# Moving the last quarter of a weight load, and its matmuls, behind the last attention unit of a decode kernel

## The chip, the cores and the metric

The kernel runs on one core of one Trainium2 chip. Times are device microseconds (us) of that core for one execution. Most executions of one kernel lie within about 1 us of each other, with now and then one 2 to 3.5 us above the fastest. So differences under half a microsecond are never read from times here, only from where instructions and transfers stand in the traces.

## The reference, cut to what matters

One decode step of a transformer block: batch 4, one new token, 32 heads of width 192, a cache of 4096 positions, model width 640, feed-forward width 1536, all bf16.

```python
q = layernorm(x) @ wq                                # 640 -> 32 x 192
p = softmax(q . k_cache * 192 ** -0.5)               # for each of 4 x 32 (batch, head)
h = x + (p @ v_cache) @ wo                           # 6144 -> 640
g = layernorm(h)
out = h + (silu(g @ w_gate) * (g @ w_up)) @ w_down   # 640 -> 1536 -> 640
```

K and V are 403 MB of the 424 MB that the kernel reads. Each byte is used once.

## The kernel before

The work is cut into 32 *units* of one batch row and four heads. A unit needs one 6.3 MB load of K and one of V. Two K buffers and one V buffer lie in on-chip memory; weights are laid over the buffers when these come free. SP (the sync engine) issues all large loads on one queue (q1, 424.29 of the 424.48 MB that the profile counts); a helper records operations with their dependences and puts the waits in. `wo` is used by *head pairs*: 16 pairs of 12 small matmuls each.

The end of the queue, in the order in which it is issued:

```python
# wo_a (pairs 0..11) over K buffer 0, wo_b (pairs 12..15) over the product buffers
for lo, hi, t, deps in ((0, WA, woA, [lambda: tk["tt", NU - 2, NQ - 1]]),
                        (WA, P, woB, [lambda: tk["red", NU - 1, NQ - 1]])):
    a = dma("sp", ... t <- wo[pairs lo..hi] ..., deps)
load_v(NU - 1)                 # last V, in four pieces, each with a semaphore of its own
k_free = [lambda: tk["tt", NU - 1, NQ - 1]]
wg_land = dma("sp", ... wgsb <- wg ..., k_free)      # gate, 2 MB
wu_land = dma("sp", ... wusb <- wu ..., k_free)      # up, 2 MB
for lo, hi in ((0, 6), (6, 10), (10, CF)):           # down, 2 MB in three pieces
    t = dma("sp", ... wdsb[:, lo:hi] <- wd ..., k_free)
```

The end of the tensor engine's (PE's) program, which PE carries out in order (queue_only, below, shows it: PE stood 12.81 us in front of one group of matmuls with the operands of the next already there):

```python
u = NU - 1
for p in range(P - 2):         # 14 head pairs: all units but the last row are done
    womm(p)
l_sum(u)
for lo, hi in VP:              # the last unit's p times V, piece by piece
    pv(u, lo, hi)
tmp(u); stt(u); o_t(u); recip(u); otm(u)     # merge, transpose, scale into OTall
womm(P - 2)                    # the two pairs that need the last unit
wo_done = womm(P - 1)
ln2 = layer_norm(psH[:, 0:DQ], [wo_done])
# ... wg's 20 matmuls [ln2, wg_land], wu's 20 matmuls [ln2, wu_land],
# ... gate product, transpose, wd's 48 matmuls by piece [wd_land], copy, output
```

## Time and profile before

| | before |
|---|---|
| time, median of 4 runs | 994.04 us (993.87 to 994.43) |
| span of the profiled execution | 992.2 us |
| mean DMA rate over the span | 428 GB/s |
| PE busy, DVE (vector engine) busy | 58%, 56% |

From the page of the profile: the span; the DMA row of the 40 slices, where 9 means 90% busy or more; the rates in those slices; and queue 1, which carries the large loads, with packets, MB and the share of 16 engines' span.

```profile
span 992.2 us, 9305 instructions
...
DMA  9999999999999999999999999999999999999997
GB/s 402 427 436 433 423 438 438 420 442 436 420 444 434 422 444 430 426 440 430 430 440 428 432 440 424 432 442 422 436 440 422 438 438 422 440 436 420 421 417 306
...
q1 hardware_dynamic: 12608, 424.29, 99.3%
q8 instruction: 7, 0.11, 0.0%
q14 instruction: 8, 0.07, 0.0%
```

The stream of loads is full from start to end, and only the last slice shows a gap. So the question for any change is what it does to the bytes or to the microseconds after the last bytes.

The last lines of the page: size of each load and microseconds from issue to landing.

```profile
wo_a<-in_A_wo_dram SPq DMA_DIRECT2D x1, 5760.0 KB, 39.5
v<-in_A_v_cache_dram SPq DMA_DIRECT2D x1, 3072.0 KB, 20.6
wo_b<-in_A_wo_dram SPq DMA_DIRECT2D x1, 1920.0 KB, 13.7
wg_sb<-in_B_w_gate_dram SPq DMA_DIRECT2D x1, 1920.0 KB, 28.7
wu_sb<-in_B_w_up_dram SPq DMA_DIRECT2D x1, 1920.0 KB, 32.1
```

The timeline of the tail: start, duration, engine, line, operation, and in brackets the engine's idle time before it and what ended it. PEld is the load of weights into PE.

```profile
946.78 0.38 SPq L365 DMA_DIRECT2D wo_b<-in_A_wo_dram  x1
947.21 3.88 SPq L354 DMA_DIRECT2D v<-in_A_v_cache_dram  x4
...
975.31 0.81 PE L455 MATMUL pb<-v,pbuf 128*8 128x384 bf16 x8 [1.37 <-DMA v<-in_A_v_cache_dram]
...
978.46 0.97 PE L495 MATMUL pb<-wo_b,OTall 128*4 128x160 bf16 x24 [0.55 <-DVE OTall L486]
...
979.48 0.33 DVE L294 BATCH_NORM_STATS2 stats<-pb 128x6 f32<-128x160 f32 x1 [0.21 <-PE pb L495]
...
982.83 1.77 PE L551 MATMUL pb<-wg_sb,lnT 128*4 128x384 bf16 x20 [1.90 <-DVE lnT L308]
...
984.49 0.10 PEld L551 LDWEIGHTS pb<-wu_sb,lnT 128*4 128x4 bf16 x8 [0.61 <-DMA wu_sb<-in_B_w_up_dram]
984.50 1.77 PE L551 MATMUL pb<-wu_sb,lnT 128*4 128x384 bf16 x20
...
987.88 1.77 PE L561 MATMUL pb<-wd_sb,guT 128*4 128x160 bf16 x48 [1.61 <-DVE guT L557]
989.70 0.33 DVE L564 CAST outsb<-pb 128x160 bf16<-128x160 f32 x1 [1.88 <-PE pb L561]
```

Issue time plus time to landing gives wo_b 946.78 + 13.7 = 960.5, wg 951.13 + 28.7 = 979.8 and wu 952.33 + 32.1 = 984.4. The reader should see two clocks running to the same point. One is work: last V, merge, `wo`, layer norm, wg's matmuls, until PE is ready for wu at about 984.5. The other is the stream, which delivers wu at 984.4. Their ends coincide.

### The profile page before, as it was taken

The numbers are of one execution on the slowest core, as the hardware profiler recorded it, in microseconds if no ns is written. First come the engines' busy times: TensorE is split into PE (matmuls) and PEld (weight loads), VectorE is DVE, ScalarE is ACT, GpSimd is POOL, SyncE is SP. The second block draws the span as 40 slices with busy tenths as digits, with TensorE's granted clock in tenths as the row PEclk, the third lists the DMA queues.
The fourth block names the chain that finished last, engine by engine and source line by source line (L and its number), as shares of the span: only waits on it lengthen the run. The fifth ranks groups of instructions, "written<-read, shape, count | busy, mean of one in ns | idle before, by whom it ended". The sixth has DMA issues, their size and how long they took to land.

```text
span 992.2 us, 9305 instructions
## 1 busy us (share of the span) xinstructions
PE 577.5 (58%) x4656; PEld 117.2 (12%) x3248; DVE 552.7 (56%) x451; ACT 108.0 (11%) x348; POOL 3.4 (0%) x19
## 2 busy tenths in 40 slices
PE   0766555676555566655557655555665555666545
PEld 0101111111001111001111100111110011110032
DVE  1486645566654556664555666455666545566602
ACT  0311111110011110001111000111100111110011
POOL 1000000000000000000000000000000000000000
PEclk9788778887777888777788877788887778887775
DMA  9999999999999999999999999999999999999997
GB/s 402 427 436 433 423 438 438 420 442 436 420 444 434 422 444 430 426 440 430 430 440 428 432 440 424 432 442 422 436 440 422 438 438 422 440 436 420 421 417 306
DMA packets 12671, 424.48 MB, mean 428 GB/s; under 512 B 1264, under 2 KB 1264, under 8 KB 3952
## 3 DMA queue, kind: packets, MB, share of 16 engines
q1 hardware_dynamic: 12608, 424.29, 99.3%
q8 instruction: 7, 0.11, 0.0%
q14 instruction: 8, 0.07, 0.0%
q10 hardware_dynamic: 48, 0.01, 0.0%
HBM read 424.29 MB, written 0.01 MB: 428 GB/s over the span
## 4 chain that ended last, share of the span: by engine, by line
DMA 67%; PE 18%; DVE 13%; SPq 1%; issue 0%; ACT 0%; DVEq 0%
DMA k<-in_A_k_cache_dram 60%; PE pb L152 11%; DVE prod L403 11%; DMA v<-in_A_v_cache_dram 8%; PE pb L455 5%; PE pb L411 2%; DVE sc L416 1%; SPq L350 0%; PE pb L551 0%; SPq L354 0%; PE pb L561 0%; PE pb L495 0%; DVE guT L557 0%; PE pb L480 0%; PE pb L298 0%
## 5 line engine op out<-in xcount | busy, mean ns | idle before, releaser
L403 DVE TENSOR_TENSOR prod<-k,qball 128x6144 f16<-128x6144 bf16 x128 | 426.3, 3351 | 200.8 <-DMA k<-in_A_k_cache_dram 200.8
L152 PE MATMUL pb<-prod,identH 128*128 128x512 f16 x1408 | 385.8, 431 | 0.0
L411 PE MATMUL pb<-prod,identH 128*128 128x512 f16 x128 | 57.9, 452 | 340.5 <-DVE prod L403 334.2
L416 DVE TENSOR_REDUCE sc<-pb 128x32 f32<-128x512 f32 x128 | 88.0, 688 | 114.0 <-PE pb L152 114.0
L455 PE MATMUL pb<-v,pbuf 128*8 128x384 bf16 x2048 | 90.8, 330 | 9.2 <-DMA v<-in_A_v_cache_dram 9.1
L461 ACT ACTIVATE otmp<-pb,mask 128x192 f32<-128x192 f32 x32 | 13.4, 420 | 678.2 <-PE pb L455 678.2
L411 PEld LDWEIGHTS pb<-prod,identH 128*128 128x128 f16 x128 | 13.2, 103 | 588.0 <-DVE prod L403 466.7
L444 ACT ACTIVATE pbuf<-sc,negM 32x128 bf16<-32x128 f32 x128 | 73.4, 574 | 2.7 <-ACT negM L438 0.2
L455 PEld LDWEIGHTS pb<-v,pbuf 128*8 128x8 bf16 x2048 | 46.8, 87 | 121.3 <-DMA v<-in_A_v_cache_dram 86.6
L465 DVE SCALAR_TENSOR_TENSOR orow<-pb,mask,otmp 128x192 f32<-128x192 f32 x32 | 13.4, 418 | 77.4 <-ACT otmp L461 77.4
L444 ACT ACTIVATION_READ_ACCUMULATOR pbuf<-sc,negM 32x1 f32 x128 | 31.7, 248 | 0.0
L480 PE MATMUL pb<-pick,orow 128*64 128x2 f32 x384 | 22.3, 231 | 2.9 <-DVE orow L465 1.0
L438 ACT ACTIVATE negM<-pb 128x4 f32<-128x4 f32 x32 | 5.5, 173 | 161.1 <-PE pb L434 161.1
L470 PEld LDWEIGHTS pb<-lsb,halfm 128*128 128x128 f32 x64 | 12.1, 190 | 72.1 <-issue 71.1
L480 PEld LDWEIGHTS pb<-pick,orow 128*64 128x64 f32 x384 | 19.6, 174 | 6.2 <-DVE orow L465 1.7
L434 PE MATMUL pb<-negMc,ones_row 1*128 1x4 f32 x64 | 12.2, 258 | 11.9 <-DVE negMc L429 11.9
L429 DVE TENSOR_REDUCE negMc<-pb 1x4 f32<-1x128 f32 x32 | 8.9, 279 | 15.1 <-PE pb L425 15.1
L425 PE MATMUL pb<-identF,msb 128*1 128x128 f32 x64 | 12.2, 271 | 8.3 <-DVE msb L421 8.2
L298 PE MATMUL pb<-mv,quadm 128*128 128x2 f32 x4 | 1.2, 364 | 23.5 <-DVE mv L296 23.5
L434 PEld LDWEIGHTS pb<-negMc,ones_row 1*128 1x128 f32 x64 | 9.4, 183 | 21.3 <-DVE negMc L429 21.3
L294 DVE BATCH_NORM_STATS2 stats<-xrow 128x6 f32<-128x160 bf16 x1 | 0.3, 327 | 17.6 <-DMA xrow<-in_A_x_dram 17.6
L495 PE MATMUL pb<-wo_a,OTall 128*4 128x160 bf16 x144 | 5.2, 335 | 7.9 <-DMA wo_a<-in_A_wo_dram 6.7
(66 smaller groups left out, 92.0 us busy)
## 6 DMA issues: line engine op xcount, KB each, us to landing
k<-in_A_k_cache_dram SPq DMA_DIRECT2D x32, 6144.0 KB, 39.9
v<-in_A_v_cache_dram SPq DMA_DIRECT2D x31, 6144.0 KB, 25.7
wq_sb<-in_A_wq_dram SPq DMA_DIRECT2D x1, 7680.0 KB, 21.2
wo_a<-in_A_wo_dram SPq DMA_DIRECT2D x1, 5760.0 KB, 39.5
v<-in_A_v_cache_dram SPq DMA_DIRECT2D x1, 3072.0 KB, 20.6
wo_b<-in_A_wo_dram SPq DMA_DIRECT2D x1, 1920.0 KB, 13.7
wg_sb<-in_B_w_gate_dram SPq DMA_DIRECT2D x1, 1920.0 KB, 28.7
wu_sb<-in_B_w_up_dram SPq DMA_DIRECT2D x1, 1920.0 KB, 32.1
```

Source lines behind the costliest of these rows:

```text
L152: return e.add_instruction(mybir.InstMatmult(name=e.bass.get_next_instruction_name(), engine=mybir.EngineType.PE, start_tensor_calc=start, ...
L403: op("dve", lambda e: e.tensor_tensor(out=prod[BUF[k]][:, :, :], in0=kslot[u % 2][:, k * QT:(k + 1) * QT, :], in1=qball[:, u, None, :].bro ...
L411: op("pe", lambda e, j=j: (e.matmul if j == 0 else partial(held_matmul, e))(psR[k][:, 0:QT * R], lhsT=identH[:, :], rhs=prod[BUF[k]][:, :, ...
L416: op("dve", lambda e: e.tensor_reduce(sc[u % 2][:, k * QT:(k + 1) * QT], psR[k][:, 0:QT * R].rearrange("q (t r) -> q t r", r=R), AX.X, ALU ...
L425: op("pe", lambda e: e.matmul(psS[0:1, XT], lhsT=msb[:, 0:1], rhs=identF[:, :], start=True, stop=True), [g("rmax", u), g("negM", u - 1), p ...
L434: op("pe", lambda e: e.matmul(psS[:, XB], lhsT=ones_row[0:1, :], rhs=negMc[0:1, :], start=True, stop=True), [g("hmax", u), g("negM", u - 1 ...
L444: op("act", lambda e, h=h, r=r: e.activation(out=pbuf[r, :, h], in_=sc[u % 2][r, :], func=ACTF.Exp, bias=negM[r, h:h + 1], scale=alpha, ac ...
L455: op("pe", lambda e, t=t, n=n: e.matmul(psO[32 * n:32 * n + 8, 0:2 * DH], lhsT=pbuf[:, t:t + 2, :].rearrange("q t m -> q (t m)"), rhs=vslo ...
L461: op("act", lambda e: e.activation(out=otmp[:, :], in_=psO[:, 0:DH], func=ACTF.Copy, scale=mask[:, 0:1]), [g("pv", u), g("stt", u - 1), km ...
L465: op("dve", lambda e: e.scalar_tensor_tensor(out=orow[:, :], in0=psO[:, DH:2 * DH], scalar=mask[:, 1:2], in1=otmp[:, :], op0=ALU.mult, op1 ...
L470: op("pe", lambda e: e.matmul(psL[:, XL], lhsT=halfm[:, :], rhs=lsb[:, :], start=True, stop=True), [g("exp", u), g("otm", u - 1)], key=("l ...
L480: op("pe", lambda e, j=j, s=s, lo=lo: e.matmul(psL[64 * s:64 * s + 64, lo:lo + 2], lhsT=orow[:, j:DH:3], rhs=pick[:, s:4:2], start=True, s ...
```

## The change

The intent: when the last V arrives behind wo_b, it arrives later than it could, by the time of wo_b's 1.97 MB (4.8 us by the landings, 955.7 to 960.5), and a long chain of work hangs on it. So the last V goes ahead of wo_b in the queue, and the matmuls of wo_b's four pairs go behind the last unit's on PE, so that they don't hold it up. The core of the diff:

```diff
-    wo_land = []
-    for lo, hi, t, deps in ((0, WA, woA, ...), (WA, P, woB, ...)):
-        ...
-    load_v(NU - 1)
+    load_wo(0, WA, woA, [lambda: tk["tt", NU - 2, NQ - 1]])
+    if LATE:
+        load_v(NU - 1)
+    load_wo(WA, P, woB, [lambda: tk["red", NU - 1, NQ - 1]])
+    if not LATE:
+        load_v(NU - 1)
...
-    for p in range(P - 2):
+    early = WA if LATE else P - 2          # 12 instead of 14
+    for p in range(early):
         womm(p)
     ...
-    womm(P - 2)
-    wo_done = womm(P - 1)
+    for p in range(early, P):
+        wo_done = womm(p)
```

Cut: the file also brings switches that are off (a faster query projection, and `LOOPS`, which rolls the unit loops of the vector and scalar engines as the PE loop already is), a new layout of OTall, `[pair, j, batch]` becoming `[unit, 2, j]`, so that the slices of OTall, which PE loads as the stationary operand of `wo`'s matmuls, are read with a step of 6 elements, and a rewritten rule for the waits inside a rolled loop. Apart from the moved operations, the order of instructions is the same on every engine.

More of the change, by code (lines that the diff above doesn't have):

```diff
@@ L12 @@
 FP16 = mybir.dt.float16
-ROLL = True
+LOOPS = False
+FASTQ = False
+LATE = True
+HELD = False
 class Cfg:
@@ L46, in __init__ @@
         self.rolled = {}
+        self.shift = 0
     def op(self, eng, fn, deps=(), key=None):
@@ L112, in body @@
                     a, n, count = at[first], at[first + 1] - at[first], last - first
-                    delta = []
+                    plan = []
                     for j in range(n):
-                        w = [waits[a + s * n + j] for s in range(count)]
-                        d = [v - w[0][m][1] for m, (_, v) in enumerate(w[1])]
-                        for s in range(count):
-                            assert at[first + s] == a + s * n
-                            assert ops[a + s * n + j].needed == ops[a + j].needed
-                            assert [(k.name, v) for k, v in w[s]] == [
-                                (k.name, v + s * d[m]) for m, (k, v) in enumerate(w[0])], (j, s, w[0], w[s])
-                        delta.append(d)
+                        w = [{k.name: (k, v) for k, v in waits[a + s * n + j]} for s in range(count)]
+                        now = []
+                        for name in sorted(set().union(*w)):
+                            k, last = w[-1][name]
+                            d = last - w[-2][name][1]
+                            v = last - (count - 1) * d
+                            assert v > 0
+                            for s in range(count):
+                                assert at[first + s] == a + s * n
+                                assert ops[a + s * n + j].needed == ops[a + j].needed
+                                assert name not in w[s] and s < 2 or w[s][name][1] == v + s * d, (eng, j, s, name)
+                            now.append((k, v, d))
+                        plan.append(now)
                     for t, w in zip(ops[:a], waits[:a]):
@@ L127, in body @@
                     with self.nc.Fori(0, count, 1, engines=bass.OrderedEngineSet([e.engine]),
-                                      head_slot={e.engine: 0}) as s:
+                                      head_slot={e.engine: 0} if eng == "pe" else None) as s:
+                        self.shift = s
                         for j in range(n):
-                            for (k, v), d in zip(waits[a + j], delta[j]):
+                            for k, v, d in plan[j]:
                                 e.wait_ge(k, s * d + v)
                             one(e, ops[a + j])
+                        self.shift = 0
                     i = a + n * count
@@ L147, in emit, with held_matmul @@
         block.sync(run("sp"))
-def held_matmul(e, out, lhsT, rhs, start, stop):
+def held_matmul(e, out, lhsT, rhs, start, stop, size=(128, 128), position=(0, 0)):
     return e.add_instruction(mybir.InstMatmult(
         name=e.bass.get_next_instruction_name(), engine=mybir.EngineType.PE, start_tensor_calc=start,
-        stop_tensor_calc=stop, tile_size=(128, 128), tile_position=(0, 0), ldweights=False,
+        stop_tensor_calc=stop, tile_size=size, tile_position=position, ldweights=False,
         ins=[e.lower_ap(rhs), e.lower_ap(lhsT, for_matmul_weights=True)], outs=[e.lower_ap(out)]))
@@ L201, in build_kernel @@
     pbuf = sb("pbuf", [128, T, 4], BF16)
-    OTall = sb("OTall", [128, P, 3, B], BF16)
+    OTall = sb("OTall", [128, NU, 2, 3], BF16)
     qsb = sb("qsb", [128, 4, 2 * DH], BF16)
-    sel = sb("sel", [128, B, 32], BF16)
+    sel = sb("sel", [128, B, 128 if FASTQ else 32], BF16)
     identF = sb("identF", [128, 128], FP32)
@@ L282, in build_kernel @@
     op("dve", lambda e: e.memset(epsv[:, :], eps))
-    ksel = op("dve", lambda e: e.tensor_copy(
-        out=sel[:, :, :], in_=r32[:, 0:B][:, :, None].broadcast_to([128, B, 32])), [c1])
+    if FASTQ:
+        ksel = op("dve", lambda e: e.tensor_copy(
+            out=sel[:, :, :].rearrange("q b (h i) -> q b h i", h=4),
+            in_=identF[:, :].rearrange("q (h r) -> q r h", h=4)[:, 0:B, :, None].broadcast_to([128, B, 4, 32])), [c2])
+    else:
+        ksel = op("dve", lambda e: e.tensor_copy(
+            out=sel[:, :, :], in_=r32[:, 0:B][:, :, None].broadcast_to([128, B, 32])), [c1])
     kquad = op("dve", lambda e: e.tensor_scalar(
@@ L321, in build_kernel @@
     qcopy = []
-    for k in range(4):
+    if FASTQ:
         for c in range(CD):
-            for n in range(4):
-                p = 2 * (4 * (k // 2) + n) + k % 2
-                a = op("pe", lambda e, k=k, c=c, n=n, p=p: e.matmul(
-                    PB[k][32 * n:32 * n + B, 0:2 * DH], lhsT=lnT[:, c, 0:B],
-                    rhs=wqsb[:, c, p * 2 * DH:(p + 1) * 2 * DH], start=(c == 0), stop=(c == CD - 1)),
-                    [ln1, wq_land, zp])
-        qcopy.append(op("act", lambda e, k=k: e.activation(
-            out=qsb[:, k, :], in_=PB[k][:, 0:2 * DH], func=ACTF.Copy, scale=1.0), [a]))
+            for k in range(4):
+                for n in range(4):
+                    rhs = wqsb[:, c, 8 * k * DH:8 * (k + 1) * DH].rearrange("q (s d) -> q s d", s=2)[:, :, n * DH:(n + 1) * DH]
+                    mm = partial(held_matmul, size=(128, 32), position=(0, 32 * n)) if k and HELD else lambda e, *a, **kw: e.matmul(*a, **kw)
+                    a = op("pe", lambda e, k=k, c=c, n=n, rhs=rhs, mm=mm: mm(
+                        e, PB[k][32 * n:32 * n + B, 0:2 * DH], lhsT=lnT[:, c, 0:B], rhs=rhs,
+                        start=(c == 0), stop=(c == CD - 1)), [ln1, wq_land, zp])
+                if c == CD - 1:
+                    qcopy.append(op("act", lambda e, k=k: e.activation(
+                        out=qsb[:, k, :], in_=PB[k][:, 0:2 * DH], func=ACTF.Copy, scale=1.0), [a]))
+    else:
+        for k in range(4):
+            for c in range(CD):
+                for n in range(4):
+                    p = 2 * (4 * (k // 2) + n) + k % 2
+                    a = op("pe", lambda e, k=k, c=c, n=n, p=p: e.matmul(
+                        PB[k][32 * n:32 * n + B, 0:2 * DH], lhsT=lnT[:, c, 0:B],
+                        rhs=wqsb[:, c, p * 2 * DH:(p + 1) * 2 * DH], start=(c == 0), stop=(c == CD - 1)),
+                        [ln1, wq_land, zp])
+            qcopy.append(op("act", lambda e, k=k: e.activation(
+                out=qsb[:, k, :], in_=PB[k][:, 0:2 * DH], func=ACTF.Copy, scale=1.0), [a]))
     wq_used = a
@@ L362, in build_kernel, with load_wo @@
             load_k(u + 2)
-    wo_land = []
-    for lo, hi, t, deps in ((0, WA, woA, [lambda: tk["tt", NU - 2, NQ - 1]]), (WA, P, woB, [lambda: tk["red", NU - 1, NQ - 1]])):
-        a = dma("sp", lambda e, lo=lo, hi=hi, t=t: e.dma_start(
+    wo_land = {}
+    def load_wo(lo, hi, t, deps):
+        a = dma("sp", lambda e: e.dma_start(
             t[:, :, :, :].rearrange("q p j n -> q p (j n)"),
             wo[lo * 2 * DH:hi * 2 * DH, :].rearrange("(p q j) n -> q p (j n)", q=128, j=3)), sem(f"s_wo{lo}"), deps)
-        wo_land += [a] * (hi - lo)
-    load_v(NU - 1)
+        for p in range(lo, hi):
+            wo_land[p] = a
+    load_wo(0, WA, woA, [lambda: tk["tt", NU - 2, NQ - 1]])
[4 more added lines that the diff above has]
+        load_v(NU - 1)
     k_free = [lambda: tk["tt", NU - 1, NQ - 1]]
@@ L383, in build_kernel @@
     qbc = {}
-    for i in range(NU // 2):
-        c = i * 2 // B
-        n, bank = c % 4, psQ[i % 2]
-        for s in range(2):
-            b = (2 * i + s) % B
-            for h in range(4):
-                k, lo = 2 * (c // 4) + h // 2, (h % 2) * DH
-                a = op("pe", lambda e, bank=bank, s=s, b=b, h=h, n=n, k=k, lo=lo: e.matmul(
-                    bank[32 * h:32 * h + 32, s * DH:(s + 1) * DH], lhsT=sel[32 * n:32 * n + B, b, :],
-                    rhs=qsb[32 * n:32 * n + B, k, lo:lo + DH], start=True, stop=True),
-                    [qcopy[k], qcopy[-1], ksel, qbc.get(i - 2)])
-        qbc[i] = op("act", lambda e, i=i, bank=bank: e.activation(
-            out=qball[:, 2 * i:2 * i + 2, :].rearrange("q u d -> q (u d)"), in_=bank[:, 0:2 * DH],
-            func=ACTF.Copy, scale=QS), [a])
+    if FASTQ:
+        for i in range(NU // 2):
+            k, b, bank = i // B, i % B, psQ[i % 2]
+            a = op("pe", lambda e, bank=bank, k=k, b=b: e.matmul(
+                bank[:, 0:2 * DH], lhsT=sel[:, b, :], rhs=qsb[:, k, :], start=True, stop=True),
+                [qcopy[k], qcopy[-1], ksel, qbc.get(i - 2)])
+            qbc[i] = op("act", lambda e, k=k, b=b, bank=bank: e.activation(
+                out=qball[:, 8 * k + b:8 * k + b + B + 1:B, :], in_=bank[:, 0:2 * DH].rearrange("q (s d) -> q s d", s=2),
+                func=ACTF.Copy, scale=QS), [a])
+    else:
+        for i in range(NU // 2):
+            c = i * 2 // B
+            n, bank = c % 4, psQ[i % 2]
+            for s in range(2):
+                b = (2 * i + s) % B
+                for h in range(4):
+                    k, lo = 2 * (c // 4) + h // 2, (h % 2) * DH
+                    a = op("pe", lambda e, bank=bank, s=s, b=b, h=h, n=n, k=k, lo=lo: e.matmul(
+                        bank[32 * h:32 * h + 32, s * DH:(s + 1) * DH], lhsT=sel[32 * n:32 * n + B, b, :],
+                        rhs=qsb[32 * n:32 * n + B, k, lo:lo + DH], start=True, stop=True),
+                        [qcopy[k], qcopy[-1], ksel, qbc.get(i - 2)])
+            qbc[i] = op("act", lambda e, i=i, bank=bank: e.activation(
+                out=qball[:, 2 * i:2 * i + 2, :].rearrange("q u d -> q (u d)"), in_=bank[:, 0:2 * DH],
+                func=ACTF.Copy, scale=QS), [a])
     BUF = (0, 1, 2, 0)
@@ L404, in tt @@
             out=prod[BUF[k]][:, :, :], in0=kslot[u % 2][:, k * QT:(k + 1) * QT, :],
-            in1=qball[:, u, None, :].broadcast_to([128, QT, DH]), op=ALU.mult),
-            [landed["k", u], qbc[u // 2], last], key=("tt", u, k))
+            in1=qball[:, bass.ds(u + 2 * pr.shift, 1), :].broadcast_to([128, QT, DH]), op=ALU.mult),
+            [landed["k", u], qbc[NU // 2 - 1 if FASTQ else u // 2], last], key=("tt", u, k))
     def red(u, k):
@@ L484, in otm @@
     def otm(u):
-        c, b = u // B, u % B
         op("dve", lambda e: e.tensor_tensor(
-            out=OTall[:, 2 * c:2 * c + 2, :, b], in0=psL[:, XO].rearrange("q (j a) -> q a j", a=2),
+            out=OTall[:, bass.ds(u + 2 * pr.shift, 1), :, :].rearrange("q u a j -> q (u a) j"), in0=psL[:, XO].rearrange("q (j a) -> q a j", a=2),
             in1=invL[:, :, None].broadcast_to([128, 2, 3]), op=ALU.mult),
@@ L495, in womm @@
                 a = op("pe", lambda e, j=j, n=n: e.matmul(
-                    psH[32 * n:32 * n + B, 0:DQ], lhsT=OTall[:, p, j, :],
+                    psH[32 * n:32 * n + B, 0:DQ], lhsT=OTall[:, p // 2 * B:p // 2 * B + B, p % 2, j],
                     rhs=w[:, p if p < WA else p - WA, j, n * DQ:(n + 1) * DQ], start=False,
@@ L502, in build_kernel @@
         pr.step("pe")
+        if u % 2 == 0:
+            pr.step("dve")
+            pr.step("act")
         for k in range(NQ):
@@ L525, in build_kernel @@
             otm(u - 1)
-    pr.step("pe")
-    if ROLL:
-        pr.roll("pe", 2, NU)
+    for eng in ("pe", "dve", "act"):
+        pr.step(eng)
+    pr.roll("pe", 1 if FASTQ else 2, NU)
+    if LOOPS:
+        pr.roll("dve", 1, NU // 2)
+        pr.roll("act", 1, NU // 2)
     u = NU - 1
     load_act = op("act", lambda e: e.activation(out=mv[:, 3:4], in_=epsv[:, 0:1], func=ACTF.Sqrt))
-    for p in range(P - 2):
+    early = WA if LATE else P - 2
+    for p in range(early):
         womm(p)
```

## The prediction

> **What bounds the kernel now.** The DMA stream. The page gives DMA queue q1 99.3% of the span and 428 GB/s over 992.2 us; the slices read 9 everywhere but in the last. [...] So only bytes, or work left after the last bytes, can matter, and the change touches no byte count.
>
> **What the tail looks like (timeline and DMA issues with their time to landing).** All big loads go through one queue and land in order of issue: wo_a (12 head pairs) 955.7, wo_b (4 pairs) 960.5, last V in four pieces 967.8, 971.5, 973.4, 975.3, wg 979.8, wu 984.4, wd in three pieces 986.7, 988.3, 989.1. After the last V piece: p·V 0.84, copy and merge 0.9, transposes 0.8, reciprocal and scale 0.4, 24 wo matmuls 1.0, layer norm 3.35 us; wg's matmuls start at 982.83, three us after wg landed. But wu's matmuls start at 984.50, when PE had waited for wu's landing (its weight loads show 0.6 us idle put down to that DMA). Then 1.8 us matmuls, gate 0.56, transpose 0.86, wd's matmuls 987.88 to 989.65, with the last eight needing a piece that landed at 989.1; copy 0.33, output about 2.2 us.
>
> **What the change does.** In the queue, the last V (6.29 MB, about 14.8 us) goes ahead of wo_b (1.97 MB, 4.8 us). [...] So: last V lands about 970.5 instead of 975.3, wo_b about 975.3, and everything behind (wg, wu, wd) where it was. The last V waits for unit 30's p·V (about 944.1) instead of the last score matmul (946.8), but wo_a was in flight until 955.7, so the earlier issue wins nothing: the queue never ran dry. On PE, 48 instead of 24 wo matmuls stand after the last unit: an estimated 1.6 us instead of 1.0. The OTall layout, the loop's wait plan and the unused branches change no instruction count or order (DVE and ACT agree one for one).
>
> **On the critical path.** New chain: V 970.5, OTall ready about 973.6, wait for wo_b to 975.3, 48 matmuls to 976.9 (before: 979.4), layer norm to 980.3, wg's matmuls to 982.1: about 2.5 us earlier. There the gain ends: wu lands at 984.4 as before, so PE waits some 2.4 us for it, and wu's matmuls start at about 984.45 instead of 984.50. The wd landing at 989.1 is a second floor. Net: 0.0 to 0.1 us.
>
> **Predicted: 993.9 us**, range 993.2 to 994.6. Faster by over 2%: 0.005; within 2%: 0.99; slower: 0.005.
>
> **What would show it.** Right: last V landing near 970.5 and wo_b near 975.3; the second layer norm starting near 977; a new idle of about 2 us before wu's matmuls put down to wu's DMA; wu's matmuls still starting near 984.4; span within 0.5 us. Wrong: a gap in the DMA share between 940 and 960; wu landing moved by over 0.5 us; wg's matmuls still near 982.8.
>
> **What would make it wrong.** A different rate of the stream (0.1% is 1 us) from the reordered reads; the slowest of the 16 engines, which lands 2.3 us after the other fifteen, catching up or falling further back; slower weight loads from the strided OTall; a different PE clock (0.5 in the tail) during the last matmuls[...].

The marks show where two sentences and a clause are cut. The sum came to 0.0 to 0.1 us less than the 994.04 us of before, which gives the 993.9 us. The 1.6 us for 48 `wo` matmuls is the estimate; 24 took 0.97 us in before.

## The result, and the profile after

| | before | after |
|---|---|---|
| time, median | 994.04 us (993.87 to 994.43, 4 runs) | 994.26 us (993.81 to 995.33, 4 runs) |
| ratio | | 1.0003, 95% interval 0.9986 to 1.0021 |
| span of the profiled execution | 992.2 us | 992.3 us |

A ratio is the mean time of one kernel's fast runs over that of the other's of the same rounds, so it isn't quite the ratio of the medians. The time is the same.

From the page of the changed kernel: span, rates and queues.

```profile
span 992.3 us, 9305 instructions
...
GB/s 408 421 436 437 423 436 440 420 440 440 418 442 438 420 442 434 422 440 438 422 440 436 424 440 428 428 444 426 430 444 424 432 444 422 434 440 424 417 418 299
...
q1 hardware_dynamic: 12608, 424.29, 99.3%
```

From its last part, the loads that answer to those above:

```profile
v<-in_A_v_cache_dram SPq DMA_DIRECT2D x1, 3072.0 KB, 18.1
wo_b<-in_A_wo_dram SPq DMA_DIRECT2D x1, 1920.0 KB, 27.7
...
wu_sb<-in_B_w_up_dram SPq DMA_DIRECT2D x1, 1920.0 KB, 32.1
```

The timeline of its tail (line numbers are those of the changed file: L503 is p times V, L542 `wo`, L605 wg and wu, L615 wd):

```profile
945.11 1.76 SPq L384 DMA_DIRECT2D v<-in_A_v_cache_dram  x4
...
947.79 0.38 SPq L396 DMA_DIRECT2D wo_b<-in_A_wo_dram  x1
...
952.49 5.75 SPq L411 DMA_DIRECT2D wu_sb<-in_B_w_up_dram  x1
...
970.68 0.81 PE L503 MATMUL pb<-v,pbuf 128*8 128x384 bf16 x8 [1.40 <-DMA v<-in_A_v_cache_dram]
...
975.49 1.77 PE L542 MATMUL pb<-wo_b,OTall 128*4 128x160 bf16 x48 [2.21 <-DMA wo_b<-in_A_wo_dram]
977.32 0.33 DVE L311 BATCH_NORM_STATS2 stats<-pb 128x6 f32<-128x160 f32 x1 [2.69 <-PE pb L542]
...
980.67 1.77 PE L605 MATMUL pb<-wg_sb,lnT 128*4 128x384 bf16 x20 [1.90 <-DVE lnT L325]
...
984.68 1.77 PE L605 MATMUL pb<-wu_sb,lnT 128*4 128x384 bf16 x20 [2.25 <-DMA wu_sb<-in_B_w_up_dram]
...
988.06 1.77 PE L615 MATMUL pb<-wd_sb,guT 128*4 128x160 bf16 x48 [1.61 <-DVE guT L611]
989.88 0.33 DVE L618 CAST outsb<-pb 128x160 bf16<-128x160 f32 x1 [1.88 <-PE pb L615]
```

Line by line against before: the last piece of V is used 4.6 us earlier (970.68 against 975.31), the layer norm starts 2.2 us earlier (977.32 against 979.48), wg's matmuls 2.2 us earlier (980.67 against 982.83). Then PE waits 2.25 us for wu, which lands at 952.49 + 32.1 = 984.6, as late as before, and wu's matmuls start 0.2 us later than before. The gain went into that new wait for wu.

### The profile page after: what moved, and what is told of

Same layout as the page of the kernel before. It is cut to its first block, busy times and chain, and to the rows that moved or that the text cites. A ratio compares the mean times of both kernels' runs of the same rounds, so it can differ in the third digit from the quotient of the medians.

```text
span 992.3 us, 9305 instructions
## 1 busy us (share of the span) xinstructions
PE 577.3 (58%) x4656; PEld 117.6 (12%) x3248; DVE 552.5 (56%) x451; ACT 108.5 (11%) x348; POOL 3.4 (0%) x19
## 3 DMA queue, kind: packets, MB, share of 16 engines
q1 hardware_dynamic: 12608, 424.29, 99.3%
## 4 chain that ended last, share of the span: by engine, by line
DMA 66%; PE 19%; DVE 13%; SPq 1%; ACT 1%; issue 0%; ACTq 0%; DVEq 0%
DMA k<-in_A_k_cache_dram 56%; PE pb L164 11%; DVE prod L451 11%; DMA v<-in_A_v_cache_dram 5%; PE pb L503 5%; DMA wu_sb<-in_B_w_up_dram 3%; DMA xrow<-in_A_x_dram 2%; PE pb L459 2%; DVE sc L464 1%; PE pb L356 1%; SPq L380 0%; ACT qball L443 0%; PE pb L439 0%; SPq L409 0%; PE pb L605 0%
## 5 line engine op out<-in xcount | busy, mean ns | idle before, releaser
L503 PE MATMUL pb<-v,pbuf 128*8 128x384 bf16 x2048 | 90.8, 330 | 4.8 <-DMA v<-in_A_v_cache_dram 4.5
L503 PEld LDWEIGHTS pb<-v,pbuf 128*8 128x8 bf16 x2048 | 46.8, 87 | 117.1 <-DMA v<-in_A_v_cache_dram 82.4
L469 DVE TENSOR_REDUCE msb<-sc 128x1 f32<-128x128 f32 x32 | 9.2, 286 | 1.1
## 6 DMA issues: line engine op xcount, KB each, us to landing
wu_sb<-in_B_w_up_dram SPq DMA_DIRECT2D x1, 1920.0 KB, 32.1
```

The lines of the kernel that those rows point to most:

```text
L503: op("pe", lambda e, t=t, n=n: e.matmul(psO[32 * n:32 * n + 8, 0:2 * DH], lhsT=pbuf[:, t:t + 2, :].rearrange("q t m -> q (t m)"), rhs=vslo ...
```

## The experiments

Twelve kernels ran, in three groups of four. The kernels of a group ran on the same chip, beside the kernel before.

### 1. Take wu away: two kernels

Kernel *nowu_before*, from the kernel before; *nowu_after* has the same edit in the changed kernel. Their outputs are wrong, which doesn't matter for the times.

```diff
-    wu_land = dma("sp", ... wusb <- wu ..., k_free)
-    for k, (w, land) in enumerate(((wgsb, wg_land), (wusb, wu_land))):
+    for k, (w, land) in enumerate(((wgsb, wg_land), (wgsb, wg_land))):
```

Expected of nowu_before:

> The kernel before, without the load of wu (the up projection reads wg's tile: a wrong result on purpose). Theory (the end was held by wu's landing at 984.4 and, at the same moment, by the layer norm chain whose wg matmuls start at 982.8): taking wu's 1.97 MB away alone gains almost nothing, because the chain behind the last V lands nowhere earlier: 993.9 us (993.3 to 994.5). Rival (the kernel is bound by its bytes to the end, so any byte less is time less): 1.97 MB at 428 GB/s is 4.6 us, so about 989.5 us.

Expected of nowu_after:

> The changed kernel, without the load of wu (wrong result on purpose). Theory: the chain that the change made 2.2 us earlier (wg's matmuls at 980.7 instead of 982.8) now runs on without a wait for wu: wg 980.7, wu's matmuls 982.3, wd's 985.9 to 987.7, about 2.1 us less: 992.0 us (991.5 to 992.6), and against the run without wu of the kernel before the change is then worth about 2 us. Rival (the change's reordering gained nothing at all on the chain, or lost it in the stream): same time as that run, near 994.

Measured: nowu_before 993.95 us (993.36 to 995.42; ratio to before 0.9999, 0.9986 to 1.0012), nowu_after 991.53 us (990.91 to 994.42; 0.9975, 0.9962 to 0.9987). The runs of before have a median of 994.20 us in this group, 993.98 in that of experiment 3 and loops_both, and 994.08 in the last.

The tail of nowu_before, from its timeline:

```profile
982.80 3.25 PE L549 MATMUL pb<-wg_sb,lnT 128*4 128x384 bf16 x40 [1.90 <-DVE lnT L308]
...
987.67 1.00 PE L559 MATMUL pb<-wd_sb,guT 128*4 128x160 bf16 x48 [1.62 <-DVE guT L555]
```

And of nowu_after:

```profile
981.01 3.37 PE L603 MATMUL pb<-wg_sb,lnT 128*4 128x384 bf16 x40 [1.90 <-DVE lnT L325]
...
986.00 1.00 PE L613 MATMUL pb<-wd_sb,guT 128*4 128x160 bf16 x48 [1.61 <-DVE guT L609]
```

What follows: 2 MB less, and the kernel before is no faster, because its work clock ends where the stream's did. (Its profiled run is the fastest of its five, and 0.6 us shorter in span than before.) With the stream's clock taken away, the change is worth 1.7 us in the profiled pair (986.00 against 987.67) and 2.4 us by the medians. So the earlier chain is real. This edit also brings every piece of wd forward by 4.2 to 4.7 us, so it takes both landings out of the way; that wu's is the first that the chain meets is read from the trace of after, where PE waits 2.25 us for wu. One thing was not expected: wd's 48 matmuls took 1.00 instead of 1.77 us in both kernels. PE's granted clock was 1.00 there, and 0.50 in the same stage of before and after. The unbroken run of matmuls ahead of wd's doesn't explain the difference: 40 run without a break in nowu_before (3.25 us), but in before too (982.83 to 986.27), and there the clock stayed at 0.50. What raised it isn't shown; both kernels of the pair have it, so it doesn't touch their difference.

### 2. Add work to the chain: two kernels

Kernels *more_before* and *more_after* move six more head pairs, 72 matmuls, behind the last unit. Results stay right.

```diff
 # more_before
-    for p in range(P - 2):
+    for p in range(P - 8):
         womm(p)
 ...
-    womm(P - 2)
-    wo_done = womm(P - 1)
+    for p in range(P - 8, P):
+        wo_done = womm(p)
 # more_after
-    early = WA if LATE else P - 2
+    early = WA - 6
```

Expected of more_before:

> The kernel before with six more head pairs (72 matmuls, about 33 ns each as the wo matmuls in the tail took) moved behind the last unit; right result. Theory: before has no slack there, so the end moves by the full 2.4 us: 996.4 us (995.6 to 997.2). Rival (PE work in the tail is hidden behind the stream as everywhere else): 994.0.

Expected of more_after:

> The changed kernel with the same six more head pairs (72 matmuls) moved behind the last unit; right result. Theory: PE waits there 1.7 us for wo_b and 2.2 us for wu, so all of it is absorbed: 994.2 us (993.6 to 994.8), the two waits shrinking by about 2.4 us together and wu's matmuls starting at 984.6 as before. Rival (the change left no slack): 996.6.

Measured: more_before 995.61 us (994.28 to 995.85; ratio 1.0007, 0.9994 to 1.0020, so not clear of 1 by times alone), more_after 993.99 us (993.80 to 994.33; 0.9996, 0.9983 to 1.0008). The start of wg's matmuls in more_before:

```profile
984.77 1.45 PE L551 MATMUL pb<-wg_sb,lnT 128*4 128x384 bf16 x16 [1.90 <-DVE lnT L308]
```

The added matmuls and the start of wu's in more_after:

```profile
972.85 2.57 PE L542 MATMUL pb<-wo_a,OTall 128*4 128x160 bf16 x72
...
984.32 1.77 PE L605 MATMUL pb<-wu_sb,lnT 128*4 128x384 bf16 x20 [2.48 <-DMA wu_sb<-in_B_w_up_dram]
```

In the traces the span of more_before is 994.0 against 992.2 us and wg's matmuls start at 984.77 against 982.83; in more_after the 72 matmuls run from 972.85 to 975.4, just as wo_b lands, and wu's matmuls start at 984.32 after a wait of 2.48 us for wu. Before had no slack, as far as its trace goes (the profiled run is the slowest of the five): most of the added work shows, about 0.5 us less than expected, since the matmuls that don't need the last unit began at 978.00, while the vector engine still scaled the last unit's result. After has slack: all of it vanishes in the wait for wo_b, which was 2.21 us and is gone. The wait for wu, which was expected to shrink too, didn't (2.48 us), so this run doesn't test the slack in front of wu.

### 3. Each half of the change alone, and neither

Kernel *queue_only*: the new order of loads with the old order of matmuls.

```diff
-    early = WA if LATE else P - 2
+    early = P - 2
```

> Half of the change: last V ahead of wo_b in the queue, but 24 of wo_b's matmuls still before the last unit's on PE. Theory: PE works in order, so the last unit's matmuls now wait for wo_b (975.4) although V is there at 970.6: p times V 975.9 to 978.7, OTall at 981.3, layer norm 982.3, wg's matmuls 985.7, and the end 2.4 us later than the full change: 996.6 us (995.6 to 997.5). Rival (the order of the loads alone is what matters, PE has room): 994.2.

Measured: 998.36 us (998.26 to 998.84), ratio 1.0042 (1.0029 to 1.0056). The direction is as expected, but the time is outside the range. From its timeline:

```profile
976.03 0.97 PE L542 MATMUL pb<-wo_b,OTall 128*4 128x160 bf16 x24 [12.81 <-DMA wo_b<-in_A_wo_dram]
976.94 0.59 PE L518 MATMUL pb<-lsb,halfm 128*128 128x2 f32 x2
977.45 3.72 PE L503 MATMUL pb<-v,pbuf 128*8 128x384 bf16 x64
```

PE stood 12.81 us in front of wo_b with the last V lying ready behind it. The miss, in terms of the chain: p times V started 1.5 us later (977.45, not 975.9), since wo_b landed at 976.0 and its matmuls and the sum came first; it took 3.72 us, not 2.8, at a granted clock of 0.50 from 976 to 978 and of 0.65 in the mean from 978 to 980 (the 64 of the unit before the last took 2.77 us in before, at 1.00); and the rest up to wg's matmuls took 6.0 us, not 7.0. That makes wg's matmuls 1.5 us later than expected (987.19, not 985.7). The two halves of the change belong together: the first without the second costs 4 us.

Kernel *matmul_only*: the old order of loads (`LATE = False`) with `early = WA`.

> The other half: wo_b still ahead of the last V in the queue, its 24 early matmuls moved behind the last unit's on PE. Theory: the chain behind the last V grows by 24 matmuls (0.8 us, 1.77 against 0.97), and before had no slack, so 0.8 us slower than before: 994.9 us (994.2 to 995.5), with wg's matmuls at 983.6 in the trace. Rival (24 matmuls more at the end are free): 994.1 and wg's matmuls at 982.8.

Measured: 993.90 us (993.70 to 994.17), ratio 0.9996 (0.9982 to 1.0010): a miss, 1 us below expectation. The timeline says why:

```profile
977.80 1.77 PE L542 MATMUL pb<-wo_b,OTall 128*4 128x160 bf16 x48
977.99 0.17 DVE L522 RECIPROCAL invL<-pb 128x2 f32<-128x2 f32 x1 [0.98 <-PE pb L528]
978.20 0.16 DVE L533 TENSOR_TENSOR OTall<-pb,invL 128x6 bf16<-128x6 f32 x1
```

The first 24 of the 48 need no result of the last unit. They start at 977.80, before the reciprocal and the scale, in the gap of 0.5 us in which PE had stood idle in before. So wg's matmuls start at 982.98 instead of 982.83, not 0.8 us later.

Kernel *riders*: the changed file with the switch off, `LATE = False`.

> The changed file with the switch of the change turned off: old order of loads and matmuls, but the new layout of OTall (weights read with a step of 6 elements) and the new wait plan of the PE loop. Theory: these cost nothing: 994.1 us (993.5 to 994.8), the 24 last wo matmuls 0.97 us as before. Rival (the reordering gains about 2 us and the strided weights or the loop eat it): 996 or so, and wo matmuls that take longer than 0.97 us.

Measured: 993.99 us (993.57 to 994.53), ratio 0.9998 (0.9984 to 1.0012), and the last 24 `wo` matmuls took 0.97 us as before. The new layout and wait plan cost nothing that shows.

### 4. What holds the stream: the vector engine's instruction transfers

The trace records 16 completions for each large load, without a name; with 16 DMA engines they are read here as one for each. In before and after, fifteen of them lie within 2.5 us, and the sixteenth falls behind in three steps. Beside it stand the 8 KB transfers of q14 in the same stretch. Both are read from the completion and transfer records of the traces:

```
us by which the slowest of the 16 completions trails the fifteenth
kernel          load landing at about   357   373   620   635   882   898   wu
before                                 0.13  0.44  0.43  1.40  1.39  2.34  2.35
after                                  0.18  0.63  0.64  1.62  1.64  2.61  2.65
loops_act                              0.09  0.42  0.43  1.40  1.35  2.31  2.34
loops_dve                              0.31  0.32  0.27  0.27  0.25  0.25  0.25
loops_both                             0.44  0.44  0.45  0.45  0.45  0.45  0.47
8 KB transfers on q14 between 200 and 950 us
before      366  430  628  748  891
after       366  428  628  750  889
loops_act   366       629       891
loops_dve        429       749
loops_both  none
```

A load counts as landed with its last completion (wu's matmuls start at 984.50, its last completion is at 984.45), so 2.35 us of wu's landing in before and 2.65 in after hang on one engine. Three kernels roll the unit loops that the changed file offers; with both rolled, q14 carries 3 transfers instead of 8:

```diff
 # loops_both
-LOOPS = False
+LOOPS = True
 # loops_dve: as loops_both, and
-        pr.roll("act", 1, NU // 2)
 # loops_act: as loops_both, and
-        pr.roll("dve", 1, NU // 2)
```

Expected of loops_both:

> The changed kernel with the vector and scalar engine's unit loops rolled, as the file already offers (fewer instructions to fetch). In both traces the slowest of the 16 DMA engines falls behind the other fifteen in three steps (0.4 us at 372, 1.0 at 635, 1.0 at 898), each within some 7 us of an 8 KB instruction transfer (366, 628, 890). Theory: those transfers are the vector engine's instructions and stall that DMA engine; without them the slowest engine stays within 0.3 us, every landing behind 898 comes about 2.4 us earlier (wu at 982.2) and the whole tail with it: 991.9 us (991.2 to 992.6). Rival (the steps have another cause, or the loops' own branches and register waits cost as much): 994.2 or more.

Expected of loops_dve:

> The changed kernel with only the vector engine's unit loop rolled. Theory: the 8 KB transfers at 366, 628 and 890 are the vector engine's instructions, those at 428 and 750 the scalar engine's; so here the first three go, the slowest DMA engine stays within about 0.5 us of the other fifteen, and the time is that of both loops rolled, 992.2 us (991.6 to 992.8). Rival (the three are the scalar engine's, or only both together matter): 994.1 and the steps stay.

Expected of loops_act:

> The changed kernel with only the scalar engine's unit loop rolled. Theory: the transfers at 428 and 750 go, but they never moved a landing, so the three steps of the slowest DMA engine stay and so does the time: 994.1 us (993.6 to 994.7). Rival: 992.2.

Measured: loops_both 992.27 us (991.70 to 993.32; ratio to before 0.9980, 0.9966 to 0.9993), loops_dve 992.58 us (991.73 to 993.69; 0.9986, 0.9972 to 1.0000), loops_act 994.36 us (994.16 to 995.83; 1.0005, 0.9991 to 1.0019). The queues of loops_both, from its page:

```profile
q1 hardware_dynamic: 12608, 424.29, 99.5%
q8 instruction: 7, 0.11, 0.0%
q14 instruction: 3, 0.02, 0.0%
```

Same bytes on q1, five fewer transfers on q14 than before (3 against 8). The table tells the rest: with the vector engine's loop rolled the three transfers at 366, 628 and 890 are gone and so are the three steps; with only the scalar engine's rolled the other two are gone, and the steps and the time stay. wu lands at 982.9 in loops_both instead of 984.6 in after (0.7 us later than expected: the last completion still trails by 0.47 us, and the fifteenth came 0.4 us later than in after), and the span is 990.6 us, 1.7 us less:

```profile
982.95 1.77 PE L605 MATMUL pb<-wu_sb,lnT 128*4 128x384 bf16 x20 [2.25 <-DMA wu_sb<-in_B_w_up_dram]
```

PE's wait for wu is as long as in after: the chain and the stream moved together.

The table counts from the fifteenth completion and so hides part of it. Sort the 16 completions of a load, count each from the first of them, and compare a load ahead of a transfer with one behind it: one of the 16 has moved. In before the three vector engine transfers move one from 1.75 to 2.74, from 2.80 to 3.77 and from 3.78 to 4.75 us, about 1.0 us each time; the first step looks like 0.3 only because that completion wasn't yet the last. The scalar engine's two transfers aren't free: they move another one from 0.67 to 1.37 and from 1.38 to 2.07 us, about 0.7 us each. But it started in the middle of the 16 and never becomes the last, so no landing waits for it. In loops_act the three steps of 1.0 us stay alone, in loops_dve the two of 0.7.

Kernel *loops_riders*: loops_both with the old order, `LATE = False`.

> Both loops rolled, but the old order of loads and matmuls. Theory: the whole tail is timed by the stream, which shifts as one, so the reordering is worth nothing here either: 992.2 us (991.6 to 992.9), within 0.3 us of both loops with the new order. Rival (with the stream 1.7 us earlier the reordered chain pays): 992.2 for the new order and about 994 for this.

Measured: 991.53 us (991.39 to 991.87), ratio 0.9973 (0.9959 to 0.9986), just below the range. The reordering gains nothing here either. But the difference to loops_both is 0.7 us, not 0.3: the two ran on different chips, and the stream itself was 0.6 us earlier in this trace (wu at 982.3). The next kernel, in the same group as this one, has the new order and comes to 991.90, and its last wd piece landed at 987.0 as here. It also splits wu, so no pair here differs in the order alone on one chip; whether the new order costs a few tenths isn't settled.

Kernel *loops_split*: loops_both with wu in two pieces.

```diff
-    wu_land = dma("sp", ... wusb <- wu ...)
+    for lo, hi in ((0, 4), (4, CD)):
+        t = dma("sp", ... wusb[:, lo:hi] <- wu ...)     # a semaphore for each
```

> Both loops rolled, the new order, and wu loaded in two pieces (four fifths, one fifth), so that most of its matmuls run before it has all landed. Theory (two floors: wu's landing, and right behind it wd's): wu's matmuls end 0.9 us earlier, but wd's last piece still lands at 987.5 with eight matmuls behind it, so PE waits there instead, and the end moves by 0.1 us at most: 992.1 us (991.5 to 992.8). Rival (wu's landing is the only floor): 0.9 us less, 991.3.

Measured: 991.90 us (991.69 to 992.11), ratio 0.9976 (0.9962 to 0.9990). From its timeline:

```profile
984.88 0.97 PE L619 MATMUL pb<-wd_sb,guT 128*4 128x160 bf16 x24 [1.61 <-DVE guT L615]
...
986.30 1.20 PE L619 MATMUL pb<-wd_sb,guT 128*4 128x160 bf16 x24 [0.45 <-DMA wd_sb<-in_B_w_down_dram]
```

The line of loops_riders to compare:

```profile
985.71 1.77 PE L615 MATMUL pb<-wd_sb,guT 128*4 128x160 bf16 x48 [1.62 <-DVE guT L611]
```

wd's matmuls begin 0.8 us earlier than in loops_riders (984.88 against 985.71), then wait for wd, and end at 987.50, as in loops_riders (985.71 + 1.77 = 987.48). The stream of wd is the second floor, right under the first. The rival's 0.9 us did not come.

So the three kernels with both loops rolled beat the kernel before by 1.7 to 2.6 us, about 0.2%, by the medians of their groups: far below the 2% that would be called faster, but with intervals below 1 for all three. It is not shown that any of the three is the best of them.

## Why the prediction was right

The number alone says little: a forecast of no change would also have come true for other reasons. What supports the mechanism are the signs that the prediction named, one by one.

- **The bound.** Right: 428 GB/s in both, 99.3% of the span on q1. Over most of before a pair of K and V loads (12.58 MB) lands every 29.07 us, which is 433 GB/s. Single slices of the page swing up to 444; it counts a whole packet where it starts, so that the DMA share of a stretch can read over 1 (1.08 from 950 to 955 us in after). The loads landed in the order of issue in both: V and wo_b changed places and the others moved by 0.2 us at most.
- **The new landings.** Right: last V at 970.6 (predicted 970.5), wo_b at 975.4 (975.3), wu at 984.6 (984.4). The last V was issued 2.1 us earlier, and that won nothing, since the stream was full at that time in both (DMA share 1.02 from 945 to 950 us in both traces).
- **The chain.** Right in kind, a little too large: 2.2 us earlier at wg's matmuls, predicted 2.5. The 48 `wo` matmuls took 1.77 us and not the estimated 1.6, and wo_b landed 0.1 us later.
- **Where the gain ends.** Right, and the step that everything rests on: the new wait for wu was 2.25 us (predicted 2.4), and without wu the change is worth about 2 us (experiment 1). Experiment 2 adds that before had no room for more work; in after the 72 extra matmuls went into the wait for wo_b, so the room in front of wu is shown by the trace and experiment 1 alone.
- **The second floor.** Borne out with the loops rolled: loops_split cut the wait for wu from 2.25 us (loops_both) to 1.38 and then waited 0.45 us for wd.
- **The slowest engine.** The prediction named it only as a risk. It is where these runs found time, and its cause was not seen: the vector engine's instruction transfers.

What stays open: why a transfer that itself lasts about 0.32 us in the records sets its engine back by 1.0 us (the vector engine's) or 0.7 us (the scalar engine's). The trace doesn't name the DMA engine of a transfer or of a completion; that each engine's transfers go to the same one every time is read from the completions above. And rolling a loop changes more than the fetching, so the transfers are shown as the cause only in so far as the steps come and go with them.

## What to carry to other kernels

In this kernel, bound by one full stream of loads, reordering loads and matmuls together moved waits and not the end; reordering the loads alone made the end 4 us later. Before costing a shorter chain, look for the next landing that the chain meets, and for the one after it; the gain is the distance to the first of them, here nothing. And look at the completions of a load one by one: the mean share of 16 engines hides one engine that is late (2.35 us for wu in before, 2.65 in after), which here was worth about 2 us where the new order was worth nothing.
